# Memory attention and feed-forward on one core: cross-partition steps of batches 2 to 7 sent through DRAM

## The chip, the core and the metric

One core of one Trainium2 chip runs the whole program. The time is the device time of one execution in microseconds. Engines: TensorE (PE, with its weight loads as PEld), VectorE (DVE), ScalarE (ACT), GpSimd (POOL) and SyncE (SP), which issues the DMAs.

## The reference

`setup_inputs()` draws q, k and v of [8 batches, 8 heads, 576 positions, 64], phi of [8, 8, 576, 32] and two weights, 512 x 2048 and 2048 x 512. All are float32 but the weights, which come as float64 and are turned into float32 in the opening (steps `i{j}` and `o{j}`, ACT and DVE).

```python
a = softmax(phi, axis=2)                          # over the 576 positions
k_m = einsum('bhsm,bhsd->bhmd', a, k)             # 32 memory keys of 64 a head
v_m = einsum('bhsm,bhsd->bhmd', a, v)
scores = (1.0 / sqrt(64)) * q @ k_m.transpose     # [576, 32] a head
attn = softmax(scores, axis=-1)
x = (attn @ v_m), heads side by side              # 4608 rows of 512
h = x @ w_in;  g = maximum(0.01 * h, h)
return g @ w_out                                  # 4608 x 512, float32
```

## The kernel before

Attention's last product and the first weight are folded: for each batch the kernel multiplies v_m by w_in (`fold_products`, steps `W{b}{j}.p`) and applies the result to the attention weights. The feed-forward part runs over groups of rows. The first groups (`G` 0 to 2) are worked in units `P`/`V`/`C`/`L`/`O` of two feature blocks, the later ones in units `p`/`v`/`s`/`c`/`l`/`d`: `p` is the up product (PE, L1118), `v` the leaky activation (ACT, L1134), `s` sums (DVE, L1155), `c` and `l` a high and a low float16 part (ACT L1159, DVE L1163), `d` the down product (PE, L1186). `x`, `z` combine and store a finished group; `z` issues four DMAs for each of its two tiles (`send`, L1053).

The order is written out by hand: `OPENING` and `LATER` are lists of step names, and each engine (SP's DMA queue too) runs its own share of a list in that order. A step that waits holds everything behind it on its engine.

A batch's attention, `attention(b, ...)`, puts partition = (head of a pair g, 64 rows) x 4 pairs `hh`. Its steps, with the engines:

- `phi`, `kv0` to `kv3`, `q0`, `q1`: loads on SP (L539, L550, L570).
- `A1` (DVE, L579): maxima of phi over 9 positions in each partition. `A2` (PE, L593) transposes them, `A3` (DVE, L600, L603) reduces over 64 partitions' values and makes two diagonals, and `B0` (PE, L609) multiplies ones by them, so that each partition has its head's maxima in PSUM (`pb`).
- `B10` subtracts them (DVE, L618), `B20` exponentiates (ACT, L624), `B3` sums (DVE, L636).
- `C10` (PE, L658) multiplies by keys and values, `C2` (PE, L672) transposes the sums, `C30` makes factors (DVE, L681 to L686). `C3k` (ACT, L693) writes the scaled keys, each row of 32 repeated three times; `C31` (DVE, L704) writes the scaled values.
- `C4` (DVE, L712, L339, L341): the values' absolute sums, their maximum in each partition and a diagonal of it. `D2` (PE, L346) multiplies ones by the diagonal; `D4` (DVE, L351 on) takes the maximum over all partitions as a power of two.
- `D10` (PE, L723): four transposes of the repeated keys, 128 x 96 each. `D3` (ACT, L740): copy to `kT`, in which partitions 0 to 31, 32 to 63 and 64 to 95 hold the same rows. `D11`, `D5`, `D6`: the values, transposed and split.
- `Q0`, `Q1` (DVE, L776): q transposed in blocks. `E1` (PE, L797): the scores, which need all three copies in `kT` and q. `E20` to `E22` (DVE, L811) and `S01` to `S08`: softmax.

Batches 0 and 1 are float32 in the fold (`b < FB`, `FB = 2`) and belong to `OPENING`.

Of the kernel before, what the change touches and what calls it, by code (L numbers as in the profile page):

```python
# [45 lines left out]
o1.y0 o1.h0 u0.O0 o1.ld1 u0.P1 a0.S17 i1.y0 o0.t1 o1.y2 u1.V1 u0.V1 i1.h0 i1.t0 i1.h1 i1.y1
i1.t1 i2.ld0 i1.y2 i1.h2 o1.y1 o1.t0 o1.h1 u1.O0 u0.O1 o1.h2 i2.ld1 o2.ld0 i1.t2 f01.1 i2.h0
i2.y0 i2.y1 a0.S18 i2.h1 i2.t1 i2.ld2 f01.2 o2.y0 o1.t1 o2.ld1 o1.t2 o2.ld2 u1.O1 i2.t0 u2.P1
o2.h0 o2.t0 u2.P0 i2.y2 i2.h2 a1.phi i2.t2 a1.kv1 a1.q0 a1.kv0 f02.1 u2.V0 u2.O0 o2.y1 o2.h1
o2.t1 u3.P1 a1.kv2 o2.y2 o2.h2 a1.kv3 a1.A1 u2.V1 u3.P0 o2.t2 i3.ld0 f02.2 a1.q1 a1.A2 a1.A3  # L50
u4.P1 a1.B0 u3.V1 u4.P0 a1.B10 u3.V0 i1.b a1.B20 u3.O0 u4.V0 u5.P0 i2.b a1.B3 a1.C10 i3.ld2
a1.Q0 i3.ld1 a1.C2 u5.V0 o0.b o1.b u2.O1 u3.O1 i3.y0 u5.P1 u4.V1 a1.C30 a1.C31 a1.C4 a1.D2 o2.b
i3.h0 a1.C3k a1.D10 a1.Q1 i3.y2 i3.h2 a1.D11 a1.D4 i3.t2 a1.D3 a1.E1 o3.ld0 a1.D5 o3.y0 i3.y1
u4.O0 i3.h1 i3.t0 u5.V1 o3.ld2 u5.O0 a1.E20 i3.t1 o3.h0 o3.t0 a1.E21 i3.b ci.1 o3.ld1 a1.E22
a1.S11 f03.1 o3.y1 a1.S01 a1.S02 a1.S03 a1.S04 u4.O1 o3.y2 o3.h2 ci.2 f03.2 a1.S12 ci.3 ci.4 e.
o3.h1 o3.t1 a1.S05 u6.P0 u6.V0 a1.S13 a1.S06 a1.S07 u6.P1 u7.P0 a1.S14 a1.S15 o3.t2 w0.2 u6.O0
a1.S16 o3.b w1.1 u7.V0 co.1 co.2 u7.O0 w1.2 co.3 u6.V1 co.4 u5.O1 o0.k0 a1.S08 o0.k1 o0.k2
u7.P1 e2. o0.l0 u7.V1 o0.l1 u6.O1 a1.S17 a1.S18 o0.l2 u7.O1
# [16 lines left out]
o1.m2 o1.s3 V12.1 o1.n2 o2.k0 C12 W13.p o2.k2 o2.l0 a2.B0 W13.h1 P13.0 W13.h0 W13.l1 P13.1
W13.l0 V13.0 o2.k1 L12 P14.0 V13.1 o2.l2 O11.0 o1.m3 o2.l1 V14.0 C13 o2.s0 P14.1 L13 o2.m0
O11.1 V14.1 o1.n3 o2.n0 o2.s1 P15.0 C14 o2.m1 O12.0 o2.s2 V15.0 o2.n1 o2.m2 L14 P15.1 o2.s3
o2.n2 O12.1 o3.k1 a2.B10 V15.1 o3.k0 o3.l1 P16.0 o3.k2 o3.l0 a2.B20 O13.0 o3.l2 V16.0 C15 o2.m3
o3.s0 a2.C10 L15 o3.s1 a2.B3 P16.1 a2.q0 O13.1 V16.1 o3.s2 C16 o3.m1 a2.q1 a2.C2 i0.l2 o3.m2
P17.0 L16 o3.m3 O14.0 o3.m0 o3.n2 V17.0 a3.phi o3.n1 o3.n3 P17.1 a2.C30 O14.1 V17.1 a2.Q0  # L80
# [6 lines left out]
W21.l1 i3.k0 o2.n3 W22.p i3.l1 V22.1 O19.1 i3.k2 i3.l0 W22.h0 W22.h1 i3.l2 P23.0 C22 W22.l0
O20.0 V23.0 L22 W22.l1 a3.A1 W23.p P23.1 W23.h0 O20.1 W23.l0 V23.1 W23.h1 os2 C23 W23.l1 a3.A2
p0.0 L23 O21.0 v0.0 a3.A3 a3.B0 p0.1 a3.B10 O21.1 v0.1 a3.B20 p0.2 a3.B3 a3.C10 v0.2 O22.0
a3.q0 a3.C2 p0.3 a3.C30 a3.q1 O22.1 v0.3 a3.C3k a3.C31 s0 c0.0 a3.D10 a4.phi l0.0 c0.1 a3.D11  # L90
p1.0 a3.Q0 p1.1 v1.0 O23.0 v1.1 a3.D3 l0.1 a3.Q1 p1.2 O23.1 v1.2 a3.C4 a4.A1 p1.3 a3.D2 v1.3
p2.0 Z2.0 p2.1 Z2.1 s1 d0.0 Z2.2 a4.A2 v2.0 d0.1 v2.1 a3.D4 c1.0 d0.2 a4.A3 c1.1 p2.2 l1.0 d0.3
# [6 lines left out]
s5 d3.5 a4.q0 d3.6 p6.0 x3.3 p6.1 l5.0 v6.0 d4.0 a4.q1 v6.1 a4.B3 c5.1 d4.1 d4.2 z3.1 p6.2 l5.1
a4.C2 v6.2 d4.3 z3.0 a5.phi d4.4 a4.C30 p6.3 a4.Q0 d4.5 v6.3 a4.C3k d4.6 s6 p7.0 c6.0 a4.D10  # L100
v7.0 l6.0 p7.1 a4.D3 d5.0 a4.Q1 v7.1 c6.1 d5.1 d5.2 l6.1 p7.2 d5.3 v7.2 a4.C31 d5.4 a5.A1 a4.E1
a4.C4 p7.3 a5.kv2 a4.E20 d5.5 v7.3 a4.D2 c7.0 s7 d5.6 a5.kv0 p8.0 p8.1 l7.0 v8.0 d6.0 v8.1
a4.E22 a5.kv3 c7.1 d6.1 a4.E21 d6.2 l7.1 a4.D11 p8.2 a5.kv1 a4.S01 d6.3 v8.2 d6.4 a4.D4 p8.3
d6.5 a4.S02 v8.3 a4.D5 W32.p s8 d6.6 W32.h0 p9.0 W32.h1 p9.1 W32.l0 v9.0 d7.0 W32.l1 v9.1 d7.1
# [1269 lines left out]
```

## Time and profile before

| what | value |
|---|---|
| median of 3 runs | 663.42 us (661.62 to 663.84) |
| span of the profiled execution, first to last instruction | 661.5 us |
| the profiled execution's own device time | not given apart; the lowest of the runs is 661.62 us |
| PE busy | 642.5 us, 97% |
| DVE busy | 522.7 us, 79% |
| ACT busy | 396.3 us, 60% |
| POOL busy | 31.7 us, 5% |
| data moved by DMA | 60.38 MB |

A row of a timeline gives start, length, engine, line and operands, and in brackets how long the engine was idle before it and for whom. A row of the groups gives how often, the busy time, the mean length in ns, and the idle time before. Matmuls are pipelined: the length of one is longer than the distance to the next start.

### The profile page before, as it was taken

The page shows a single profiled execution, that of the slowest core. Times are in us where ns is not written, and L with a number is a line of the kernel's source. Part 1 is how long each engine was busy: PE and PEld are TensorE (multiplying, and loading weights), DVE is VectorE, ACT ScalarE, POOL GpSimd, SP SyncE. Part 2 cuts the span into 40 slices and gives each one's busy share as a digit, 9 for nine tenths or more (in the row PEclk, how much of TensorE's full clock was granted, in tenths as well). Part 3 has the DMA queues.
Part 4 walks back from the last instruction along what each step waited for, and adds up shares of the span by engine and source line. Part 5 has one row for each costly group of instructions (what it writes and reads, how often), then busy time and mean ns, then how long its engine had stood idle before and what let it go on. Part 6 is the DMA issues. An engine that isn't in the chain of part 4 may idle for free.

```text
span 661.5 us, 17591 instructions
## 1 busy us (share of the span) xinstructions
PE 642.5 (97%) x7592; PEld 482.2 (73%) x7592; DVE 522.7 (79%) x857; ACT 396.3 (60%) x677; POOL 31.7 (5%) x43
## 2 busy tenths in 40 slices
PE   6899999999999999999999999999999999999996
PEld 3345445665545787888888889887888888889883
DVE  5775789999994998989898965888877997575641
ACT  2797878674652655566546665655665466564552
POOL 0010021000110001001000020000010001000000
PEclk9799999999999999999999999999999999999999
DMA  9989803104601443611161101054104010100101
GB/s 251 406 334 323 277 3 95 63 1 110 190 1 38 116 149 73 172 43 33 39 182 68 34 1 33 8 136 146 33 1 106 2 34 7 28 25 11 33 2 48
DMA packets 31453, 60.38 MB, mean 91 GB/s; under 512 B 4240, under 2 KB 14480, under 8 KB 31376
## 3 DMA queue, kind: packets, MB, share of 16 engines
q1 hardware_dynamic: 31280, 59.13, 29.6%
q8 instruction: 59, 0.97, 0.6%
q10 hardware_dynamic: 96, 0.13, 0.1%
q14 instruction: 18, 0.15, 0.1%
HBM read 49.81 MB, written 9.44 MB: 90 GB/s over the span
## 4 chain that ended last, share of the span: by engine, by line
PE 86%; DVE 8%; DMA 2%; ACT 1%; issue 1%; SPq 0%; DVEq 0%; ACTq 0%
PE po L1186 30%; PE ph L1118 20%; PE po L1075 13%; PE ph L1007 7%; PE ph L1186 5%; PE pa L913 4%; DMA arena<-in_q_dram 2%; PE pa L797 2%; PE pa L658 2%; PE po L1220 1%; DVE arena L776 1%; DVE arena L1163 1%; DVE w_mem L952 1%; PE pa L1276 1%; DVE arena L443 0%
## 5 line engine op out<-in xcount | busy, mean ns | idle before, releaser
L1186 PEld LDWEIGHTS <-arena 128*128 128x128 f16 x2184 | 209.9, 98 | 33.2 <-issue 10.3
L1134 ACT ACTIVATE wi<-ph,g_sc 128x256 f32<-128x256 f32 (+1 forms) x224 | 99.2, 465 | 178.5 <-PE ph L1118 175.5
L1118 PE MATMUL ph<-a,w_mem 128*128 128x256 f16 (+3 forms) x1440 | 145.3, 246 | 0.7 <-ACT wi L1134 0.5
L1118 PEld LDWEIGHTS <-w_mem 128*128 128x128 f16 x1440 | 114.6, 98 | 14.3 <-issue 3.4
L1186 PE MATMUL po<-wo,arena 128*128 128x256 f16 x936 | 122.2, 273 | 1.2 <-issue 1.2
L1186 PE MATMUL po<-arena 128*128 128x256 f16 x936 | 122.2, 273 | 0.0
L1075 PE MATMUL po<-wo,arena 128*128 128x512 f16 (+1 forms) x384 | 111.1, 434 | 0.4 <-DVE arena L1028 0.4
L1163 DVE TENSOR_TENSOR arena<-arena 128x1024 f16<-128x1024 f32 x52 | 63.9, 1228 | 23.8 <-ACT arena L1159 23.7
L1163 DVE TENSOR_TENSOR arena<-wi,arena 128x768 f16<-128x768 f32 (+1 forms) x60 | 53.6, 893 | 10.1 <-ACT arena L1159 10.1
L1155 DVE TENSOR_TENSOR arena<-wi 128x256 f32<-128x256 f32 x104 | 41.0, 436 | 24.3 <-ACT wi L1134 23.0
L1159 ACT CAST arena<-arena 128x1024 f16<-128x1024 f32 x52 | 54.5, 1047 | 5.9 <-DVE arena L1155 5.9
L1007 PE MATMUL ph<-a,w_mem 128*128 128x192 f16 (+2 forms) x304 | 52.2, 317 | 0.7 <-DVE a L856 0.7
L1075 PEld LDWEIGHTS <-arena 128*128 128x128 f16 x288 | 27.7, 98 | 30.3 <-DVE arena L1028 0.9
L1159 ACT CAST arena<-wi 128x768 f16<-128x768 f32 (+1 forms) x60 | 46.6, 776 | 1.6
L1155 DVE TENSOR_TENSOR arena<-wi,arena 128x256 f32<-128x256 f32 x104 | 45.8, 440 | 1.8
L880 POOL TENSOR_TENSOR a<-t,a 128x384 f16<-128x384 f32 x22 | 24.1, 1120 | 438.2 <-ACT a L875 438.2
L1186 PE MATMUL ph<-wo,arena 128*128 128x256 f16 x312 | 42.6, 273 | 0.0
L1075 PEld LDWEIGHTS po<-wo,arena 128*128 128x128 f32 x96 | 17.7, 190 | 21.4 <-issue 19.0
L913 PE MATMUL pa<-wi,vT 64*32 64x512 f16 (+1 forms) x704 | 28.9, 420 | 0.4 <-ACT vT L746 0.4
L1014 ACT ACTIVATE arena<-ph,g_sc 128x384 f32<-128x384 f32 x32 | 18.4, 576 | 16.7 <-PE ph L1007 16.6
L1007 PEld LDWEIGHTS <-w_mem 128*128 128x128 f16 x240 | 20.7, 98 | 9.4 <-issue 3.4
L776 DVE STREAM_TRANSPOSE arena<-arena 96x1536 f32<-96x1536 f32 x14 | 24.8, 1768 | 3.1 <-PE pa L658 2.6
(204 smaller groups left out, 771.7 us busy)
## 6 DMA issues: line engine op xcount, KB each, us to landing
arena<-in_q_dram SPq DMA_DIRECT2D x16, 576.0 KB, 6.5
out_dram<-obs SPq DMA_DIRECT2D x142, 64.0 KB, 1.7
arena<-in_k_dram SPq DMA_DIRECT2D x28, 288.0 KB, 4.9
arena<-in_v_dram SPq DMA_DIRECT2D x28, 288.0 KB, 5.1
arena<-in_moe_w_in_dram SPq DMA_DIRECT2D x12, 512.0 KB, 9.1
arena<-in_moe_w_out_dram SPq DMA_DIRECT2D x8, 768.0 KB, 6.7
arena<-in_phi_dram SPq DMA_DIRECT2D x7, 576.0 KB, 5.5
arena<-in_moe_w_in_dram SPq DMA_DIRECT2D x8, 256.0 KB, 8.3
```

The costliest lines, as they stand in the source:

```text
L776: nc.vector.transpose(flat, ld["q", g].rearrange("p hh j d -> p (hh j d)"))
L880: nc.gpsimd.tensor_tensor(lo[:, tb], t2[:, tb], hi[:, tb], ALU.subtract)
L913: nc.tensor.matmul(pf[g][cols, :], lhs, rhs, start=(n == 0), stop=(n == len(passes) - 1), tile_position=(g * D, hh * M),)
L1007: nc.tensor.matmul(ph[:, t0:t0 + n * SB], lhs, rhs, start=(m == 0), stop=(m == len(seq) - 1))
L1014: nc.scalar.activation(dst, ph, AF.Prelu, scale=sc, alpha=SLOPE)
L1075: nc.tensor.matmul(po, lhs, rhs, start=(f == 0 and m == 0), stop=(f == NQ * NF - 1 and m == len(seq) - 1),)
L1118: nc.tensor.matmul(ph[:, t0:t0 + n], lhs, rhs, start=(m == 0), stop=(m == len(seq) - 1))
L1134: nc.scalar.activation(dst, ph, AF.Prelu, scale=g_sc2[:, j:j + 1], alpha=SLOPE)
L1155: nc.vector.tensor_tensor(gt[:, x], y, z, op)
L1159: nc.scalar.copy(dst[:, 0], src)
L1163: nc.vector.tensor_tensor(dst[:, 1], src, dst[:, 0], ALU.subtract)
L1186: nc.tensor.matmul(acc, g[:, x, s, u], rhs, start=(h == 0 and j == 0 and u == 0 and m == 0), stop=(j == NQ - 1 and u == 1 and m == 2), ski ...
```

## The change

For batches 2 to 7 (`far`) three things cross partitions otherwise; batches 0 and 1 keep the old steps, and `OPENING` holds the same steps in the same order.

```diff
+    dram = ctx.enter_context(tc.tile_pool(name="dram", bufs=2, space=bass.MemoryType.DRAM))
...
+    def max_row(src):
         m = sm.tile([P, 1], F32, name="m1")
         nc.vector.tensor_reduce(m, src, AX.X, ALU.max)
+        return m
+
+    def max_diag(src):
+        m = max_row(src)
         diag = sm.tile([P, P], F32, name="mdiag", bufs=1)
         nc.vector.tensor_scalar_mul(diag, ident, m)
         return diag
...
+        far = b >= FB
...
+        if far:
+            @step("A2")
+            def _():
+                t = att.tile([P, HP, 32], F32, name="r1k", bufs=2)
+                nc.vector.transpose(
+                    t.rearrange("p hh x -> p (hh x)"), var["mx"].rearrange("p hh m -> p (hh m)")
+                )
+                var["mx4"] = mx4 = sm.tile([P, HP], F32, name="mx4")
+                nc.vector.tensor_reduce(mx4, t, AX.X, ALU.max)
+
+            @step("A4")
+            def _():
+                d = dram.tile([P, HP], F32, name="d_mx")
+                nc.sync.dma_start(d, var["mx4"])
+                var["mb"] = mb = att.tile([P, 2 * M * HP], F32, name="r1k", bufs=2)
+                for g in range(NG):
+                    row = d[g * D:(g + 1) * D].rearrange("p (o hh) -> o (p hh)", o=1)
+                    nc.sync.dma_start(
+                        mb[g * D:(g + 1) * D], row.broadcast_to([D, 2 * M * HP])
+                    )
+
+            @step("A3")
+            def _():
+                two = var["mb"].rearrange("p (i m hh) -> p i hh m", i=2, hh=HP)
+                var["pb"] = pb = att.tile([P, HP, M], F32, name="r1k", bufs=2)
+                nc.vector.tensor_tensor(pb, two[:, 0], two[:, 1], ALU.max)
+        else:
...
         @step("C3k")
         def _():
-            var["x_k"] = x_k = att.tile([P, NG, ND, NB, 32], F32, name="x_k")
+            x_k = att.tile([P, NG, ND, NB, 32], F32, name="x_k")
+            if far:
+                both = x_k.rearrange("p g db tb x -> p (g db tb x)")
+                var["x_k"], var["kS"] = both[:, 0:P], both[:, P:2 * P]
+                for g in range(NG):
+                    nc.scalar.activation(
+                        var["x_k"][:, g * D:(g + 1) * D], var["pk"][g][:, 0:D], AF.Copy,
+                        scale=var["r2"][:, 1, g:g + 1],
+                    )
+                return
+            var["x_k"] = x_k
...
-            var["vdiag"] = max_diag(l1)
+            if far:
+                var["m1"] = max_row(l1)
+            else:
+                var["vdiag"] = max_diag(l1)
...
         @step("D10")
         def _():
+            if far:
+                var["pkT"] = ps_a.tile([P, P], F32, name="pa")
+                nc.tensor.transpose(var["pkT"], var["x_k"], ident)
+                return
...
-        @step("D2")
-        def _():
-            var["pm"] = spread(var["vdiag"])
-
-        @step("D3")
-        def _():
-            var["kT"] = kT = att.tile([CP, NG, ND, P], F32, name="kT")
-            nc.scalar.copy(kT, var["pkT"])
+        if far:
+            @step("C5")
+            def _():
+                d = dram.tile([P, 1], F32, name="d_m1")
+                nc.sync.dma_start(d, var["m1"])
+                var["pm"] = sm.tile([P, P], F32, name="mdiag", bufs=1)
+                nc.sync.dma_start(
+                    var["pm"], d.rearrange("(o p) x -> o (p x)", o=1).broadcast_to([P, P])
+                )
+
+            @step("D3")
+            def _():
+                nc.scalar.copy(var["kS"], var["pkT"])
+
+            @step("D12")
+            def _():
+                d = dram.tile([P, P], F32, name="d_k")
+                nc.sync.dma_start(d, var["kS"])
+                var["kT"] = kT = att.tile([CP, NG, ND, P], F32, name="kT")
+                for tb in range(NB):
+                    nc.sync.dma_start(
+                        kT[tb * 32:(tb + 1) * 32],
+                        d.rearrange("(g db x) c -> x g db c", g=NG, db=ND),
+                    )
+        else:
...
```

So `A2` becomes a block transpose and a reduction on DVE; `A4` writes 128 x 4 numbers to DRAM and reads each head's 256 of them into its 64 partitions; `A3` becomes one maximum of 128 columns; `B0` is gone. `C4` loses its diagonal, `C5` writes 128 numbers and reads all of them into every partition, and `D2` is gone. `C3k` writes each key row once, `D10` is one transpose of 128 x 128, `D3` copies its 128 columns to SBUF, and `D12` writes them to DRAM (64 KB) and reads them into `kT` three times. All nine DMAs of a batch are on SP.

`LATER` is a new list of the same steps besides these. The stretches from before `D10` to `E1` in batches 4, 5 and 6, as they now read:

```
batch 4: ... a4.B3 c5.1 d4.1 l5.0 d4.2 v6.1 z3.1 d4.3 p6.2 l5.1 a4.C2 v6.2 a5.phi d4.4 a4.C30 p6.3
  a4.Q0 os3 d4.5 z3.0 v6.3 a4.C31 a4.C3k d4.6 a4.D10 s6 p7.0 c6.0 l6.0 p7.1 a4.D3 a4.D12 d5.0 a4.Q1
  v7.0 v7.1 c6.1 d5.1 d5.2 p7.2 d5.3 v7.2 l6.1 d5.4 a5.A1 p7.3 a4.E1 a4.C4 a4.C5
batch 5: ... z5.1 a5.B3 d12.1 z5.0 d12.2 p14.2 d12.3 v14.2 a5.C2 d12.4 a6.phi p14.3 a5.C30 d12.5 a5.Q0
  v14.3 s14 a5.C3k a5.Q1 p15.0 a5.D10 a5.D3 c14.0 d12.6 l14.0 c14.1 v15.0 p15.1 a5.C31 d13.0 l14.1
  v15.1 a5.D12 d13.1 d13.2 d13.3 p15.2 p15.3 v15.2 a5.C4 a5.C5 a6.A1 d13.4 a5.E1
batch 6: ... a6.C3k d25.4 p27.3 a6.C4 a6.C5 a6.D10 v27.3 c27.0 l26.1 s27 a6.D11 d25.5 a6.D3 a6.D12
  d25.6 l27.0 c27.1 p28.0 a6.D4 p28.1 v28.0 d26.0 v28.1 a6.D5 d26.1 a6.Q1 d26.2 p28.2 p28.3 d26.3
  d26.4 a6.D6 v28.2 a7.A1 a6.E1
```

Elsewhere the list moves steps by a few places, `A3` comes after `A2` and `A4` with other DVE steps in between, and `D4` likewise after `C4` and `C5`.

More of the change, by code (lines that the diff above doesn't have):

```diff
@@ L46 @@
[L46 to L57, printed above, removed]
@@ L75 @@
[L75 to L80, printed above, removed]
@@ L87 @@
[L87 to L92, printed above, removed]
@@ L99 @@
[L99 to L104, printed above, removed]
@@ L184 @@
+d52.0 z15.0 z15.1 p54.1 d52.1 v54.1 p54.2 c54.0 d52.2 v54.2 l54.0 p54.3 d52.3 v54.3 p55.0 c54.1
+d53.0 l54.1 v55.0 p55.1 d53.1 v55.1 p55.2 c55.0 d53.2 l55.0 v55.2 p55.3 d53.3 v55.3 d54.0 c55.1
+l55.1 d54.1 d54.2 d54.3 d55.0 d55.1 d55.2 d55.3 end
 """
@@ L588, in attention @@
             steps[f"{name}A1"] = lambda: max_phi(0, HP)
-        @step("A2")
-        def _():
-            var["pt"] = pt = ps_a.tile([P, NG, D], F32, name="pa")
-            nc.tensor.transpose(
-                pt.rearrange("p g x -> p (g x)"), var["mx"].rearrange("p hh m -> p (hh m)"), ident
-            )
-        @step("A3")
-        def _():
-            mx2 = sm.tile([P, NG], F32, name="mx2")
-            nc.vector.tensor_reduce(mx2, var["pt"], AX.X, ALU.max)
-            var["diag"] = diag = att.tile([P, NG, P], F32, name="r1k", bufs=2)
-            for g in range(NG):
-                nc.vector.tensor_scalar_mul(diag[:, g, :], ident, mx2[:, g:g + 1])
```

263 lines of the change are left out of this document (151 added, 112 removed).

## The prediction

> **What bounds the kernel now.** I read the page's busy times and its chain first, then the stages, then the instructions around each piece that the change takes away.
>
> ```profile
> span 661.5 us, 17591 instructions
> PE 642.5 (97%) x7592; PEld 482.2 (73%) x7592; DVE 522.7 (79%) x857; ACT 396.3 (60%) x677; POOL 31.7 (5%) x43
> PEclk9799999999999999999999999999999999999999
> PE 86%; DVE 8%; DMA 2%; ACT 1%; issue 1%; SPq 0%; DVEq 0%; ACTq 0%
> ```
>
> The core's time by stages (busy time of PE, PEld, DVE, ACT, POOL, then clock, DMA share, GB/s):
>
> ```profile
> 104.00:170.00 66.00, 65.57 (x688) 39.85 (x687) 64.75 (x96) 44.07 (x72) 0.22 (x2) 1.00 0.30 86
> 290.00:350.00 60.00, 59.72 (x870) 51.56 (x868) 53.64 (x87) 36.55 (x64) 3.75 (x4) 1.00 0.31 86
> ```
>
> TensorE (PE) is busy for 65.57 of 66 and 59.72 of 60 us at full clock, and 86% of the chain is PE. From 104 us on, where batches 2 to 7 are worked, an instruction taken from PE's order is worth the distance to the next start, and whatever makes PE wait costs its full length. VectorE (DVE) is as full only from 104 to 170 us (64.75 of 66).
>
> **What PE loses.** PE's timeline, batch 7 first, then the same steps in batches 4, 5 and 6 (start, length, line):
>
> ```profile
> 477.88 0.27 PE L593 MATMUL pa<-ident,r1k 128*128 128x128 f32 x1
> 477.99 0.82 PE L1186 MATMUL po<-arena 128*128 128x256 f16 x6
> ...
> 482.78 0.44 PE L609 MATMUL pa<-r1k,ones 128*64 128x128 f32 x4
> 483.15 0.83 PE L1186 MATMUL po<-arena 128*128 128x256 f16 x6
> ...
> 512.75 0.60 PE L723 MATMUL pa<-ident,x_k 128*96 128x128 f32 x4
> 513.18 1.47 PE L1186 MATMUL po<-arena 128*128 128x256 f16 x12
> 514.49 0.49 PE L1118 MATMUL ph<-a,arena 128*128 128x256 f16 x3
> 514.82 0.49 PE L1118 MATMUL ph<-a,obs 128*128 128x256 f16 x3
> 515.74 0.49 PE L346 MATMUL pa<-mdiag,ones 128*128 128x128 f32 x2 [0.42 <-DVE mdiag L341]
> ...
> 268.95 0.60 PE L723 MATMUL pa<-ident,x_k 128*96 128x128 f32 x4
> 269.68 0.81 PE L1118 MATMUL ph<-a,w_mem 128*128 128x256 f16 x6
> ...
> 336.54 0.60 PE L723 MATMUL pa<-ident,x_k 128*96 128x128 f32 x4
> 337.42 0.81 PE L1118 MATMUL ph<-a,w_mem 128*128 128x256 f16 x6 [0.28 <-ACT wi L1134]
> ...
> 345.28 0.39 PE L346 MATMUL pa<-mdiag,ones 128*128 128x128 f32 x2
> 345.50 0.27 PE L731 MATMUL pa<-ident,x_v 128*128 128x128 f32 x1
> ...
> 440.17 0.62 PE L723 MATMUL pa<-ident,x_k 128*96 128x128 f32 x4
> 441.00 0.46 PE L346 MATMUL pa<-mdiag,ones 128*128 128x128 f32 x2 [0.21 <-DVE mdiag L341]
> ```
>
> Matmuls overlap, so I price by starts, not by lengths. A2 (one transpose) holds PE for 477.99 - 477.88 = 0.11 us. B0 (two products, four instructions) holds it for 483.15 - 482.78 = 0.37. D10 (four transposes) holds it for 0.43; one stays at 0.11, so 0.32 goes. D2 holds it for 345.50 - 345.28 = 0.22 where nothing disturbs it. Together 0.11 + 0.37 + 0.32 + 0.22 = 1.02 us a batch, 6.1 us over six batches.
>
> With D2 goes its wait for DVE's diagonal. In batch 7 three products started 0.33 apart from 514.49 to 514.82, so D2 could have started at 515.15 and did at 515.74: 0.59 lost. In batch 6 four transposes from 440.17 should end at 440.60 and D2 starts at 441.00: 0.4. I add 0.2 for the other four and take 1.2 us in all, zero and 1.5 as ends. After D10 in batch 5, PE stands 337.42 - 336.54 - 0.43 = 0.45 us behind ScalarE (ACT), which is busy with the copies of the keys; in batch 4 it is 269.68 - 268.95 - 0.43 = 0.3. The lighter copies below should win back about half of these 0.75: 0.4, ends 0 and 0.75. What PE gains: 6.1 + 1.2 + 0.4 = 7.7 us, ends 6.1 and 8.4.
>
> **DVE and ACT.** Groups by line and shape:
>
> ```profile
> L600 DVE TENSOR_REDUCE mx<-pa 128x2 f32<-128x128 f32 x8 | 2.2, 280 | 1.1 <-PE pa L593 1.1
> L603 DVE TENSOR_SCALAR r1k<-ident,mx 128x128 f32<-128x128 f32 x16 | 3.9, 284 | 0.4
> L341 DVE TENSOR_SCALAR mdiag<-ident,m 128x128 f32<-128x128 f32 x8 | 2.3, 287 | 0.3
> L811 DVE STREAM_TRANSPOSE t<-pa 128x384 f32<-128x384 f32 x24 | 12.7, 560 | 0.8 <-PE pa L797 0.6
> L712 DVE TENSOR_REDUCE l<-x_v 128x2 f32<-128x128 f32 x8 | 2.0, 254 | 0.0
> L693 ACT ACTIVATE x_k<-pa,r 128x192 f32<-128x192 f32 x14 | 5.1, 417 | 0.3 <-DVE r L686 0.3
> L740 ACT COPY kT<-pa 96x512 f32<-96x512 f32 x8 | 4.6, 578 | 2.0 <-PE pa L723 2.0
> L746 ACT COPY vT<-pa 128x128 f32<-128x128 f32 x2 | 0.5, 264 | 0.2 <-PE pa L731 0.2
> ```
>
> DVE drops the reduction of 280 ns, two diagonals of 284 and one of 287: 1.14 us a batch. It gains a transpose of 128 columns, a reduction like L712's (254), and a maximum of 128 columns like L603's (284). The transpose lies between a third of L811's 560 and all of it; I take 300, so 0.84 us. DVE is lighter by 0.3 us a batch. B1 (the subtraction) and the reduction in D4 only read another place; I cost that at nothing. On ACT two copies of 417 ns shrink to 64 columns (at least L746's 264 halved, at most 417; I take 300), and D3 goes from 578 to L746's 264: 0.55 us a batch. Neither engine is on the path after 170 us, so none of this enters the sum beyond the 0.4 above.
>
> **The round trips.** Nothing in this trace writes to DRAM and reads back, so each hop is bounded by its nearest row: stores of 64 KB for the write, input loads of 288 KB for the read.
>
> ```profile
> L1053 SPq DMA_DIRECT2D out_dram<-obs x142: 314/422/1871, 105.1 to 658.2; - x142
> ...
> DMA to landing us min/median/max: 1.6/1.7/3.6
> ...
> L550 SPq DMA_DIRECT2D arena<-in_k_dram x28: 328/384/1805, 48.5 to 451.3; - x28
> ...
> DMA to landing us min/median/max: 2.7/5.3/11.5
> ```
>
> A write: 1.7 us (1.6 to 3.6). A read of at most 64 KB: above a store's 1.6, below 2.7, the quickest load of 288 KB; I take the middle, 2.2, with 5.3 as the far end if small reads fare like loads. Each issue holds the SP queue for 0.42 us. So A4 (write, two reads) lasts 1.7 + 0.4 + 2.2 = 4.3 us, C5 (write, one read) 3.9, D12 (write, three reads) 1.7 + 0.8 + 2.2 = 4.7. SP serves its list in order: while it waits for a write, all later loads and stores stand behind it. Per batch that is some 1.7 us three times and nine issues of 0.42. In the rows below SP issues eight stores and a load and has nothing to do before and after, and loads are listed long before their use, so I cost that at nothing; if a load became late, its reader on DVE would wait by as much.
>
> A3 and D4 make DVE wait for A4 and C5. Batch 3 has the closest A3, with about 4.6 us of DVE work listed after A2 against 4.3. Batch 6 has the closest D4, about 3.7 against 3.9 behind C4. D5 on ACT follows D4, so a late bound also holds activations there. What hides small misses is DVE's lead over PE:
>
> ```profile
> 338.33 1.23 DVE L1163 TENSOR_TENSOR arena<-arena 128x1024 f16<-128x1024 f32 x1
> ...
> 347.60 0.82 PE L1186 MATMUL ph<-wo,arena 128*128 128x256 f16 x6
> ```
>
> This operand is ready at 339.56 and its products start at 347.60, 8 us later. If that lead were gone, each miss would cost its length.
>
> E1 makes PE itself wait for D12. Counting PE's blocks (twelve products of 256 take 514.49 - 513.18 = 1.31 us above, so six take 0.66) between D10 and E1 in the new order gives the cover: 8.8 us in batch 2, 13.8 in 3, 5.9 in 4, 5.9 in 5, 7.3 in 6, 10.6 in 7. Batches 2, 3 and 7 cover the 4.7 us and the copies before it. The others also have the next phi load just ahead on the same queue:
>
> ```profile
> 331.45 4.75 SPq L1053 DMA_DIRECT2D out_dram<-obs x8
> 336.31 0.41 SPq L539 DMA_DIRECT2D arena<-in_phi_dram  x1
> ...
> 435.90 0.39 SPq L539 DMA_DIRECT2D arena<-in_phi_dram  x1
> ```
>
> Batch 5: eight stores and phi end on SP at 336.7, 0.2 us after D10. D12's write then goes out at about D10 + 0.8, right behind 576 KB, so I give it the slow 3.6: landed at 4.4, last read at 4.4 + 0.8 + 2.2 = 7.4, cover 5.9: 1.5 us lost. Batch 4: phi is earlier, but four stores (z3.0, 1.7 us) come between and a cast of ACT stands before D3: write at 1.4, landed at 3.6 (2.2, mild traffic), last read at 6.6: 0.7 lost. Batch 6: SP has C5 before D12. Phi left at D10 - 4.3; C4 ends at about D10 + 0.5, C5's write takes 2.1 (phi is nearly in) and lands at 2.6, its read is out at 3.0, D12's write lands at 4.8, last read 7.8 against 7.3: 0.5 lost. Sum 2.7 us; ends 0 and 2.7 + 3 x 3.1 = 12 (reads of 5.3).
>
> **Sum.** 661.5 - 7.7 + 2.7 = 656.5 us of span. The median of the runs shown, 663.42, is 1.9 above the span; what lies around the span and the scatter of 661.62 to 663.84 make this up. So 658.4 us, 0.8% faster. A difference of 0.3% (2 us) is what a measurement can tell here.
>
> **Rivals.** (1) All round trips are hidden, since the reads land in 1.6 to 1.9 us and the phi load doesn't delay the writes. Then the whole 7.7 to 8.4 us shows: 655.0 to 655.7. For it: undisturbed stores land in 1.7 and the misses are all under 1.5. Against: the 3.6 among the stores. (2) The other side: the reads fare like loads, E1 becomes the new stop of PE, and the kernel is slower. With 5.3 us a read, batches 4, 5 and 6 lose 9.3 more: 667.7. It cancels the gain at 2.2 + 5.0 / 3 = 3.9 us a read. For it: the reads pass the same 16 engines as phi, and loads take 5.3 in the median. Against: those are 288 KB each and up to eight in a row. (3) In between, reads of about 3.7 us leave no difference: 662.9. (4) DVE is the bound from 104 to 170 us, so batch 2's 1.0 us doesn't appear: 659.4, inside the first case's range; DVE's lighter load speaks against it.
>
> The stores' spread from 1.7 to 3.6 is what rival 2 rests on. [...]
>
> **How the numbers follow.** Forecast 0.56 (own range 656.0 to 661.3), rival 1 0.23, rival 3 0.12, rival 2 0.09. Faster 0.56 + 0.23 = 0.79, same 0.12, slower 0.09. The range starts at 654.0, a little under rival 1, and ends at 663.0, which leaves out rival 2 and some of both edges.
>
> **What would show it.** PE's busy time falls by about 6 us and L346, L593 and L609 keep only batches 0 and 1. L723's counterpart is one transpose a far batch. E1's first matmul shows a wait for a DMA of about 1.5 us in batch 5 and under 1 in 4 and 6. Small reads land in about 2.2 us, writes in 1.7. DVE shows short waits for DMA at A3 and D4, without PE waiting after them. The prediction is wrong if reads take 4 us or more, if a far E1 waits over 3 us, or if the new order makes PE wait at places that have nothing to do with the round trips.

## The result and the profile after

The changed kernel takes 696.75 us in the median (695.55 to 697.21) beside 663.45 us (661.62 to 663.84): ratio 1.0509, 95% interval 1.0484 to 1.0535. It is 33 us slower, outside the range and on the other side of no change. The profiled execution spans 694.8 us. From its page, the span, the busy times, the granted clock by slices and the beginning of the chain:

```profile
span 694.8 us, 17550 instructions
PE 651.2 (94%) x7532; PEld 484.9 (70%) x7532; DVE 517.1 (74%) x851; ACT 390.6 (56%) x677; POOL 32.1 (5%) x43
PEclk9999999999999999999999999997999989999999
PE 67%; DMA 13%; DVE 12%; ACT 4%; issue 2%; another core or an unknown queue 1%; SPq 1%; POOL 0%; DVEq 0%; ACTq 0%; POOLq 0%
```

PE runs 60 instructions fewer (7592 to 7532), as the change says, and yet is busy for 8.7 us more (642.5 to 651.2). Fewer products are busy for longer if they run at a lower clock (six of 128x256 take 0.82 us from 346.35 on, at a clock of 1.00, and 1.49 from 476.04 on, at 0.50), and the clock row has two dips in the middle that were not there before. (A slice is 17 us long. Seen more finely, by windows of the trace, the granted clock is at 0.50 or 0.51 in five stretches: 3.4 us each from 235.9, 300.8 and 352.0 us on, 10.2 from 468.0 and 6.8 from 553.3.) The chain, 86% PE, 8% DVE and 2% DMA before, now has 67% PE, 13% DMA and 12% DVE. So there are two losses: PE waits, and afterwards it is slow.

The DMA issues of the new steps (KB each, and the median time from issue to landing in us):

```profile
r1k<-d_mx SPq DMA_DIRECT2D x12, 64.0 KB, 2.8
kT<-d_k SPq DMA_DIRECT2D x18, 64.0 KB, 1.9
d_k<-x_k SPq DMA_DIRECT2D x6, 64.0 KB, 3.3
d_mx<-mx SPq DMA_DIRECT2D x6, 2.0 KB, 1.8
mdiag<-d_m SPq DMA_DIRECT2D x6, 64.0 KB, 5.6
d_m<-m SPq DMA_DIRECT2D x6, 0.5 KB, 7.2
```

The maxima and the keys are near their forecast: writes 1.8 and 3.3 us, reads 2.8 and 1.9. The odd pair is C5's, and its odd member is the smallest transfer of the list: 512 bytes take 7.2 us to be written, and reading them back takes 5.6. With the issue of the read in between, C5 lasts about 13 us.

Who waits for it, from the list of who waited for whom (us in total, times, longest):

```profile
DVE pv L352 <- DMA mdiag<-d_m: 26.6, 5, 7.9
ACT vT L832 <- DVE sv L826: 24.9, 5, 7.6
PE ph L1189 <- ACT wi L1205: 11.4, 9, 3.8
PE pa L868 <- DVE vT L837: 5.7, 1, 5.7
PE pa L868 <- DMA kT<-d_k: 4.8, 1, 4.8
```

This is one wait handed on. DVE stands at D4 (L352), ACT behind it at D5 (L832), and PE behind ACT's next activations or behind D6 (L837). Batch 7 in the timeline (start, length, engine, line; in brackets the idle time before and what ended it):

```profile
541.03 0.38 SPq L783 DMA_DIRECT2D d_m<-m  x1
...
547.71 0.51 PE L868 MATMUL pa<-arena,kT 32*32 32x192 f32 x4
548.27 0.34 SPq L785 DMA_DIRECT2D mdiag<-d_m  x1
552.03 0.29 DVE L352 TENSOR_REDUCE pv<-mdiag 128x1 f32<-128x128 f32 x1 [7.87 <-DMA mdiag<-d_m]
...
552.92 0.37 ACT L832 ACTIVATE vT<-pa,sv 128x128 f16<-128x128 f32 x1 [7.65 <-DVE sv L826]
553.55 0.34 DVE L837 SCALAR_TENSOR_TENSOR vT<-pa,sv,vT 128x128 f16<-128x128 f32 x1
553.94 0.53 PEld L868 LDWEIGHTS pa<-arena,kT 32*32 32x32 f32 x29 [6.10 <-DVE vT L837]
```

C5's write goes out at 541.03 and its read only 7.24 us later. E1 starts at 547.71 and stops after four products: its next score tile needs a `ps_a` buffer that D11's `px` holds until D5 and D6 have read it, and these wait for the bound. PE stands for 6 us for a number that it doesn't use.

The stretch with that wait and the one behind it, and the same for batch 6 (busy time of PE, PEld, DVE, ACT, POOL, then clock, DMA share, GB/s):

```profile
465.00:471.00 6.00, 1.18 (x10) 0.65 (x7) 2.27 (x5) 1.45 (x4) 0.00 (x0) 0.75 0.18 53
471.00:476.00 5.00, 5.00 (x102) 3.23 (x101) 3.80 (x8) 0.48 (x1) 0.00 (x0) 0.50 0.31 79
...
548.00:553.50 5.50, 0.22 (x4) 0.00 (x0) 1.32 (x5) 0.58 (x2) 0.00 (x0) 0.99 0.04 12
553.50:560.50 7.00, 6.56 (x110) 4.51 (x110) 5.14 (x12) 1.35 (x3) 0.00 (x0) 0.52 0.01 2
```

After each long wait PE is fully busy again, at a clock of 0.50 and 0.52. That is where the extra busy time comes from.

### The profile page after: what moved, and what is told of

It is laid out like the page before. It is cut to its first block, busy times and chain, and to the rows that moved or that the text cites. A ratio compares the mean times of both kernels' runs of the same rounds, so it can differ in the third digit from the quotient of the medians.

```text
span 694.8 us, 17550 instructions
## 1 busy us (share of the span) xinstructions
PE 651.2 (94%) x7532; PEld 484.9 (70%) x7532; DVE 517.1 (74%) x851; ACT 390.6 (56%) x677; POOL 32.1 (5%) x43
## 4 chain that ended last, share of the span: by engine, by line
PE 67%; DMA 13%; DVE 12%; ACT 4%; issue 2%; another core or an unknown queue 1%; SPq 1%; POOL 0%; DVEq 0%; ACTq 0%; POOLq 0%
PE po L1257 24%; PE ph L1189 17%; PE po L1146 8%; DMA d_m<-m 5%; PE ph L1078 5%; PE ph L1257 4%; PE pa L984 4%; PE pa L687 2%; DMA mdiag<-d_m 2%; DMA arena<-in_moe_w_in_dram 2%; DVE arena L847 2%; PE pa L868 1%; PE po L1291 1%; DMA arena<-in_moe_w_out_dram 1%
## 5 line engine op out<-in xcount | busy, mean ns | idle before, releaser
L1257 PEld LDWEIGHTS <-arena 128*128 128x128 f16 x2184 | 213.0, 99 | 34.9 <-issue 9.0
L1189 PE MATMUL ph<-a,w_mem 128*128 128x256 f16 (+3 forms) x1440 | 147.0, 248 | 10.5 <-ACT wi L1205 10.5
L1189 PEld LDWEIGHTS <-w_mem 128*128 128x128 f16 x1440 | 116.0, 99 | 26.0 <-issue 13.9
L1257 PE MATMUL po<-wo,arena 128*128 128x256 f16 x936 | 126.4, 279 | 0.0
L1146 PEld LDWEIGHTS <-arena 128*128 128x128 f16 x288 | 27.8, 98 | 33.3 <-issue 4.1
L1226 DVE TENSOR_TENSOR arena<-wi,arena 128x256 f32<-128x256 f32 x104 | 43.8, 421 | 1.8
L984 PE MATMUL pa<-wi,vT 64*32 64x512 f16 (+1 forms) x704 | 30.4, 428 | 1.7 <-ACT vT L817 1.2
L868 PE MATMUL pa<-arena,kT 32*32 32x192 f32 x672 | 18.0, 383 | 12.4 <-DVE vT L837 5.7
L1017 ACT ACTIVATE w_mem<-pa 128x512 f16<-128x512 f32 x40 | 22.4, 595 | 9.8 <-PE pa L984 8.9
L1023 DVE SCALAR_TENSOR_TENSOR w_mem<-pa,w_mem 128x512 f16<-128x512 f32 x40 | 26.3, 680 | 0.9 <-ACT w_mem L1017 0.9
```

What stands on the lines that cost most here:

```text
L868: nc.tensor.matmul(psc[tb][cols, g, :], var["kT"][rows, g, db, cols], var["qT", g][rows, hh, :, db, :], start=(db == 0), stop=(db == ND - ...
L984: nc.tensor.matmul(pf[g][cols, :], lhs, rhs, start=(n == 0), stop=(n == len(passes) - 1), tile_position=(g * D, hh * M),)
L1023: nc.vector.scalar_tensor_tensor(tiles(t[:, 1]), w(g), ws, tiles(t[:, 0]), ALU.mult, ALU.subtract)
L1146: nc.tensor.matmul(po, lhs, rhs, start=(f == 0 and m == 0), stop=(f == NQ * NF - 1 and m == len(seq) - 1),)
L1189: nc.tensor.matmul(ph[:, t0:t0 + n], lhs, rhs, start=(m == 0), stop=(m == len(seq) - 1))
L1226: nc.vector.tensor_tensor(gt[:, x], y, z, op)
```

## The experiments

Three terms are used throughout. "Waits of PE" are the sum of all gaps over 0.25 us between the starts of two products beyond the first one's own length, from 104 us to the end: 15.7 us before and 44.3 after. The sum also counts the length of small products that start side by side, so only its differences between kernels mean something; the profile's own list of PE's waits adds up to some 5 us before and 8 in versions 1 and 5, which is the same difference. "Order of before" and "new order" are the two lists `LATER`. "Version 3" is the kernel of experiment 3, and so on.

**1. Bound back on PE.** The changed kernel and its order, without C5 and with D2 again:

```
-            @step("C5")
-            def _():
-                d = dram.tile([P, 1], F32, name="d_m1")
...
+            @step("D2")
+            def _():
+                var["pm"] = spread(var["vdiag"])
```

> The changed kernel with v's bound back on TensorE (D2 and the diagonal instead of C5); maxima and keys still go through DRAM, and the new order stays. Theory A: the bound's round trip (write 7.2 us, read 5.6 us in the trace of after) is the whole loss, by DVE and ACT standing in D4 and D5, then PE, then the halved clock. Then 663.4 - 6 x (0.11 + 0.37 + 0.32) = 658.6 us plus up to 3 us of waits in E1: 657 to 662, mean granted clock 0.99. Rival B: the three trips and the new order share the loss. Then at least 672 us, and clock under 0.985.

Measured: 662.3 us (660.87 to 664.05), ratio 0.9999 (0.9979 to 1.0019), 0.3 us above theory A's range and 10 below rival B's. Without C5 all 33 us are gone. The trips of the maxima and of the keys, in the same order, cost nothing net, but the 4.8 us of PE work that they save (0.11 + 0.37 + 0.32, six times) don't show either. Waits of PE are 19.3 us, 3.6 more than before, the largest group of them this:

```profile
PE ph L1190 <- ACT wi L1206: 4.4, 6, 2.1
```

None of them names a DMA. ACT is late at places where the new order has put other work of ACT or DVE ahead.

**2. The bound alone.** The order of before and all of its steps, with C5 right behind C4 and D2 gone, for instance in batch 3:

```
-a3.C4 a4.A1 p1.3 a3.D2 v1.3
+a3.C4 a3.C5 a4.A1 p1.3 v1.3
```

> The kernel before, in its own order, with one part of the change: v's bound through DRAM, C5 right behind C4, no D2. Theory A: about the whole loss appears: 685 to 700 us, clock 0.97 to 0.98, D4 waiting some 5 us a batch. Rival B: 675 us or less.

Measured: 706.5 us (704.67 to 707.93), ratio 1.0665 (1.0636 to 1.0694), beyond the range of theory A too. The order of before leaves even less between C4 and D4: DVE stands at D4 for 40.5 us, beside 26.6 in the changed kernel. Waits of PE are 52.2 us, and the largest is the buffer of `px` again:

```profile
PE pa L869 <- DVE vT L838: 17.0, 3, 7.7
```

**3. The bound used later.** The changed kernel, its order altered alone: C5 behind D12, and D4 to D6 (in batches 3, 6 and 7 also D11 and the fold products) at least 13 us of PE work behind C4, for instance in batch 2:

```
-... C18 Z1.2 O16.0 a2.D11 a2.S01 ... a2.S02 i1.k1 a2.D4 a3.kv1 ... a2.D5 P20.0 ... a2.D6
+... a2.D12 a2.C4 a2.C5 P18.1 ... a2.D11 a2.S01 ... O18.0 a2.D4 a2.D5 a2.D6 i1.l1 a2.S08
```

> The changed kernel with all three trips, and only the order altered: C5 stands behind D12 on SP, and D4, D5, D6 (with D11 and the fold's W steps in batches 3, 6 and 7) come at least 13 us of PE work behind C4. Theory A says that what hurts is the wait behind too short a cover: 656 to 661 us and clock 0.99. Rival C: SP itself, held 7 us a batch by the slow write, delays loads, stores and E1, so that even a covered trip costs: at least 668 us.

Measured: 671.8 us (667.81 to 673.88), ratio 1.0153 (1.0123 to 1.0182). With nearly the same trip (writes of 6.2 us, reads of 5.4) merely covered, 25 of the 33 us are back, and in the profiled execution no slow stretch of the clock is left in the middle. The forecast of full cover was too good, and the time lies where rival C had put it. The trace doesn't bear C out: SP does stand behind C5's writes for 39.5 us, but after 104 us no wait of PE, DVE or ACT for a DMA is longer than 0.3 us. Waits of PE are 27.8 us, and they have moved to the steps that I had shifted, ACT first:

```profile
PE ph L1190 <- ACT wi L1206: 8.1, 12, 2.1
PE pa L764 <- ACT x_k L725: 2.0, 1, 2.0
```

The profiled execution took 667.81 us at a mean clock of 0.997; the other three took 671.60 to 673.88 at 0.988 to 0.994. What made them 4 to 6 us longer is not in a trace, and stays open.

**4. The trips by themselves.** A kernel of write and read pairs on an otherwise empty chip, each behind the one before, four times over. It leaves out the reference's whole computation. The form of rows of 4 bytes:

```
+        nc.sync.dma_start(d[:, 0:src_cols], src)
...
+            row = d[0:n].rearrange("p x -> (p x)").rearrange("(o y) -> o y", o=1)
+            nc.sync.dma_start(t, row.broadcast_to([P, dst]))
```

> Leaves out the whole computation: only hops through DRAM, one after another on an otherwise idle queue, four times each: 128 rows of 4, 8, 16, 64 and 512 bytes, 4-byte rows at a pitch of 64 and 512 bytes, four rows of 4 bytes, one row of 512 bytes, each read back. Theory A1 (row size): 4-byte rows land in about 7 us at any pitch, 16-byte rows in about 1.8. Theory A2 (rows that share a block of memory): 4-byte rows land in about 7 us when packed and about 2 at a pitch of 512 bytes; 8-byte rows lie between. Rival A3 (the kernel's own traffic): all land in 1.5 to 2.5 us here. For the reads: one row of 512 bytes read by all 128 partitions takes 4 to 6 us if the shared source slows it, 2 if traffic did.

From its list of DMA issues (128 rows written each time; 0.5 KB are rows of 4 bytes, 1.0 KB of 8, 2.0 KB of 16, packed without a gap; `w4at` are rows of 4 bytes at a distance of 64 or 512 bytes; `t_one` is one row of 512 bytes read into 128 partitions, `t_f` one of 16 bytes; the 64 KB `t_w` are four reads of 128 different rows of 512 and four of C5's form). The last number is the median of the landings on record, one or two of the four of most forms; that of the 64 KB `t_w` is of 128 different rows:

```profile
t_w<-d_w SPq DMA_DIRECT2D x8, 64.0 KB, 1.8
...
t_one<-d_one SPq DMA_DIRECT2D x4, 64.0 KB, 3.1
d_w4at<-s_w4at SPq DMA_DIRECT2D x8, 0.5 KB, 1.4
...
d_w<-s_w SPq DMA_DIRECT2D x4, 0.5 KB, 6.9
d_w<-s_w SPq DMA_DIRECT2D x4, 1.0 KB, 3.0
d_w<-s_w SPq DMA_DIRECT2D x4, 2.0 KB, 2.2
...
t_f<-d_f SPq DMA_DIRECT2D x4, 2.0 KB, 2.5
```

The write is slow without any traffic, so theory A3 (contention) falls. It isn't the size of a row either (A1): rows of 4 bytes take 6.9 us packed and 1.4 us at a distance of 64 bytes. It is how close the rows lie in DRAM (A2): of 128 rows, 16 to every 64 bytes cost 6.9 us, 8 rows 3.0, one row 1.4. With 4 rows the 2.2 is a single landing; by the start of the read behind it, four of five such writes took 1.4 us and one 2.2. A short row as such costs nothing here: by the same measure rows of 4 bytes at a distance took 1.4 us, rows of 64 bytes 1.4 and rows of 512 bytes 1.5. Why close rows are slow, no run shows. What the trace does show is where the time lies (DVE, POOL, clock, DMA share, GB/s):

```profile
53.28:54.48 1.20, 0.00 (x0) 0.00 (x0) 1.00 0.06 0
54.48:60.28 5.80, 0.00 (x0) 0.00 (x0) 1.00 0.00 0
```

The packed write was issued at 53.28 and the read that waits for it at 60.29. The DMA engines have work for it only in the first 1.2 us, at a share of 0.06; for the other 5.8 us their share is 0.00 and the write is still awaited. The same number of rows at a distance, issued at 90.15, was over after 1.4. So neither the number of rows nor work of the DMA engines that the trace shows makes the difference. On the read side one shared source row takes 3.1 us where 128 different rows of the same size take 1.8.

**5. Four rows instead of 128.** The changed kernel and its order, with the bound reduced before it leaves the chip: DVE spreads the row maxima over 32 columns, turns the 32x32 blocks and takes the maximum again, and C5 carries 4 numbers.

```
-                var["m1"] = max_row(l1)
+                m1 = max_row(l1)
+                nc.vector.tensor_scalar_mul(w[:, 0:32], ones[:, 0:32], m1)
+                nc.vector.transpose(w[:, 32:64], w[:, 0:32])
+                nc.vector.tensor_reduce(w[:, 64:65], w[:, 32:64], AX.X, ALU.max)
...
-                nc.sync.dma_start(d, var["m1"])
+                nc.sync.dma_start(d, var["w"][0:P:32, 64:65])
```

> The changed kernel with its order, but v's bound made compact before it leaves the chip: VectorE spreads the 128 row maxima over 32 columns, turns the 32x32 blocks, and takes the maximum again, so that one value stands for each block of 32 rows; C5 then writes 4 rows of 4 bytes and reads one row of 16 bytes into every partition. Three short VectorE instructions a batch are added. Theory (packed 4-byte rows are slow to write and one 512-byte row shared by 128 partitions is slow to read, and nothing else of C5 costs): in the bare trips such a write took about 1.6 us and such a read about 2.5 us, so C5 ends 4 to 5 us after C4 instead of 13, PE's long waits around D4 to D6 go, the granted clock is 0.99 again, and the time is 659 to 665 us, that is at or a little below the 662 of the version with the bound on PE. Rival (the place of the D4 to D6 steps in the new order is wrong for any trip through DRAM, however short): waits of 2 to 4 us stay and the time is 675 us or more.

Measured: 660.95 us (659.49 to 661.86), ratio 0.9969 (0.9952 to 0.9987), 0.3% faster than before, 36 us faster than the changed kernel. Its page and its new DMAs:

```profile
span 658.0 us, 17568 instructions
PE 635.1 (97%) x7532; PEld 477.4 (73%) x7532; DVE 520.5 (79%) x869; ACT 391.4 (59%) x677; POOL 31.9 (5%) x43
PEclk9999999999999999999999999999999999999999
...
mdiag<-d_m SPq DMA_DIRECT2D x6, 2.0 KB, 2.7
```

This gives the cleanest account of the loss, because PE has the same 7532 instructions as in the changed kernel. The spans differ by 694.8 - 658.0 = 36.8 us. Of these, 651.2 - 635.1 = 16.1 are PE's busy time, the same products at a lower clock (some 3 of it in the opening, where the clock is 0.97 up to 104 us in the changed kernel, while version 5's mean over its whole span is 1.000), and 20.7 are PE's idle time. DVE, with three more instructions a batch, has nothing to say in it.

**6. The pause by itself.** 21 groups of float16 products with ScalarE copies between them, for which the next group waits. It leaves out the reference's whole computation. `n` goes from 1 to 8000 and back:

```
+        for _ in range(GROUP):
+            nc.tensor.matmul(acc, w, r, start=True, stop=True)
...
+            nc.scalar.copy(x[:, 0:1], acc[:, 0:1])
+            nc.scalar.copy(y[:, 0:n], x[:, 0:n])
+            nc.scalar.copy(r[:, 0:1], y[:, 0:1])
```

> This measures the granted clock after a pause of TensorE by itself and leaves the reference's whole computation out: 21 groups of 160 float16 products of 128x512 (about 35 us each), and between them ScalarE copies that the next group waits for, from a bare 0.5 us to about 8 us, once in rising and once in falling order. Theory H (a pause of 2.8 us and more, not the work around it, halves the clock afterwards): no half-clock stretch behind pauses under about 2 us, a stretch of 3.4 us or more behind every pause above 3 us, longer behind the longest. Rival (the half clock of the changed kernel comes with what its other engines do, not with the pause): full clock throughout, whatever the pause.

Pauses are given from one start to the next, 0.2 us of which is the first product. No slow stretch followed those of 0.63 to 2.24 us; of the two of 2.8 us one was followed by one, of the two of 3.41 us one, and from 3.99 us on every one. Each slow stretch behind a pause was 3.4 or 6.8 us long. How equal pauses differ shows in stretches of 3.4 us laid on the edges of the slow ones (columns as above):

```profile
197.10:200.50 3.40, 1.05 (x5) 0.39 (x4) 0.00 (x0) 2.25 (x3) 0.00 (x0) 1.00 0.00 0
200.50:204.00 3.50, 3.41 (x9) 1.19 (x9) 0.00 (x0) 0.04 (x1) 0.00 (x0) 0.51 0.00 0
234.60:238.00 3.40, 2.32 (x11) 0.98 (x10) 0.00 (x0) 1.01 (x2) 0.00 (x0) 1.00 0.00 0
238.00:241.50 3.50, 1.55 (x8) 0.72 (x8) 0.00 (x0) 1.86 (x2) 0.00 (x0) 1.00 0.00 0
```

The pause of 2.83 us lay in one stretch, left PE busy for 1.05 of 3.40 us in it, and the next stretch ran at 0.51. The pause of 3.41 us lay across two, left 2.32 and 1.55, and neither was followed by a slow one. That the place of a pause between such edges decides is my reading. It fits the changed kernel, whose slow stretches of 3.4, 6.8 and 10.2 us start 64.9, 51.2, 116.0 and 85.3 us apart, to 0.1 us 19, 15, 34 and 25 times 3.41. There less than 2.83 us was enough: PE idle for 2.10 us, at p15.1, all of them in one stretch. Version 5 has the same 2.10 us idle, from 333.57 to 335.67, of which 1.97 lie in the stretch of the last row:

```profile
348.50:351.95 3.45, 1.35 (x13) 1.07 (x11) 3.42 (x6) 2.29 (x4) 0.00 (x0) 1.00 0.60 183
351.95:355.40 3.45, 3.45 (x19) 2.46 (x17) 3.35 (x6) 0.13 (x1) 0.00 (x0) 0.51 0.27 60
...
333.70:337.10 3.40, 1.43 (x14) 1.28 (x14) 3.37 (x7) 2.15 (x4) 0.00 (x0) 1.00 0.53 174
```

The first two rows are of the changed kernel, the last of version 5, where the 3.4 us behind it ran at 1.00. So for these two waits the border lies near 1.4 us of work in 3.4, and one of the five slow stretches stands behind a wait that isn't C5's. PE's busy time alone isn't the whole measure. In the changed kernel the two longer slow stretches go on behind 3.4 us with PE busy for 3.41 us (from 471.42 on) and 2.81 (from 553.34 on), almost all of it E1's 32*32 products at a clock of 0.50; and in the opening a slow stretch stands behind 1.51 us (from 24.27 on), and before the change one behind 2.19 (from 14.33 on). The rival, other engines' work as the cause, falls, since here the slow stretches come with DVE, POOL and the DMA at 0.00.

**7. Where the saved PE work goes.** Single parts of the change in the order of before. The maxima alone (A4 behind A2, A3 right ahead of B10), for instance in batch 5:

```
-v12.2 a5.A2 d10.4 ...
+v12.2 a5.A2 a5.A4 d10.4 ...
...
-d11.0 a5.B10 v13.1
+d11.0 a5.A3 a5.B10 v13.1
```

> The kernel before with its own order and one part of the change alone: in batches 2 to 7 phi's maxima go through DRAM (A2 writes follow A1, A4's reads follow A2, A3 stands right ahead of B10, B0's products are gone). Theory O (the trips of the maxima are hidden, and what the version with the bound on PE lost, it lost in waits that the new order makes): the 2.9 us of PE work saved shows, 660.0 to 661.5 us, ratio 0.995 to 0.998, and PE's waits after 104 us stay within 1 us of the 15.7 us of before. Rival D (the trips by DMA themselves make new waits, whatever the order): 662.5 us or more, and waits of PE on A3 or B10.

Measured: 663.41 us (661.78 to 665.61), ratio 1.0011 (0.9998 to 1.0024): theory O falls for this part. PE is rid of 2.9 us and waits 3.6 us more, at C10 (L687), behind the exponentials that the later A3 makes late. In batches 3 and 5 A3 itself is late because DVE waits there for A4's reads, so that here, as rival D has it, the trip is too long for its place:

```profile
PE pa L687 <- ACT arena L653: 2.4, 2, 1.9
...
DVE r1k L617 <- DMA r1k<-d_mx: 5.4, 2, 3.0
```

The keys alone, and both. In these two the delayed scores of batches 2, 4, 5 and 6 come behind loads of the next batch into the queries' area, so that part of the scores is made from other data. Batch 4, the same in both:

```
-a4.D3 d5.0 ... a5.A1 a4.E1 a4.C4 p7.3 a5.kv2 a4.E20 d5.5
+a4.D3 a4.D12 d5.0 ... a5.A1 a4.C4 p7.3 a5.kv2 d5.5 v7.3 c7.0 s7 d5.6 a5.kv0 p8.0 a4.E1 p8.1 a4.E20
```

> The kernel before with its own order and one part of the change alone: in batches 2 to 7 the repeated rows of keys go through DRAM (D12 right behind D3); the scores from E1 on, and the D steps that stand behind E1 in batches 2, 4, 5 and 6, are put 1.3 to 4.6 us of PE work later, so that at least 6.5 us lie between D3 and E1. Theory O (hidden trips, a loss only by the new order): the 1.9 us of PE work saved shows, 661.0 to 662.5 us, ratio 0.996 to 0.999. Rival D (the trips or the later scores make new waits): 663 us or more, with PE waiting at E1 on kT's transfers.

> The kernel before with its own order and two parts of the change: maxima and keys through DRAM as in the two kernels run beside it, v's bound left on PE. Theory O: the two gains add up, 658 to 660.5 us, ratio 0.993 to 0.997; this would be the best version so far. Rival D: within 0.3% of before, as the same two parts were in the new order (662.3 us beside 662.25).

Measured: 678.54 us (ratio 1.0234, 1.0211 to 1.0257) and 677.41 us (1.0230, 1.0209 to 1.0252). The waits on those loads are in these times, so they say nothing of the trips. The keys alone once more, with the loads behind E1, in batch 4 (against the list above):

```
-p7.3 a5.kv2 d5.5 v7.3 c7.0 s7 d5.6 a5.kv0 p8.0 a4.E1 p8.1 a4.E20
+p7.3 d5.5 v7.3 c7.0 s7 d5.6 p8.0 a4.E1 a5.kv2 p8.1 a4.E20 a5.kv0
```

> The kernel before with its own order and the keys alone through DRAM, as in the run of the keys before, with one difference: the loads of the next batch's keys and values, which share an area with this batch's queries, stay behind E1. In the two runs with keys in the old order they had come ahead of it, so that the scores of batches 2, 4, 5 and 6 were partly made from the next batch's data and E1 waited for those loads. Theory O (hidden trips; what is lost is lost by an order that puts late work before PE): 661.0 to 663.0 us, within 0.3% of before or a little under, PE's waits at E1 below 1 us each. Rival D (the trip or the later scores cost PE more than the 1.9 us saved): 664.5 us or more.

Measured: 668.75 us (668.20 to 669.23), ratio 1.0088 (1.0070 to 1.0106). Slower, as rival D has it, but not where it looked: PE doesn't wait at E1 at all. It waits at the fold products (L985), since D4 to D6 had to move behind the later E1:

```profile
PE pa L985 <- DVE vT L838: 2.7, 1, 2.7
```

This wait leaves PE busy for 1.05 us of the 3.4 from 185.20 on, and the next 3.4 us run at a clock of 0.50. So no single part pays when it is put into the order of before by hand. What a trip needs is room, and in a full order the room is taken from another step.

**8. The short bound in the order of before.** The list of version 2 with the lines of version 5:

> The kernel before with its own order and one part alone: v's bound through DRAM in the four-row form, C5 right behind C4 where the 512-byte form cost 44 us. Theory (it was the length of the trip, 13 us beside 4 to 5): 660 to 665 us; about 2.5 us of PE work saved, at most some 1 to 2 us lost in batches 3, 6 and 7, where D4 follows C4 within 2.7 to 4.9 us of PE work. Rival (any trip through DRAM at this place costs PE): 675 us or more.

Measured: 664.78 us (663.55 to 667.10), ratio 1.0036 (1.0023 to 1.0050): 42 us less than version 2, with C5 at the same place. It was the length of the trip. It still costs 0.4% there, at scores that wait until D6 has read `px`:

```profile
PE pa L873 <- DVE vT L842: 2.7, 3, 1.8
```

**9. Four steps moved.** Version 5, with batch 4's C3k and D10, v15.0 and batch 7's C10 moved by a few places:

```
-d4.4 a4.C30 p6.3 a4.Q0 os3 d4.5 z3.0 v6.3 a4.C31 a4.C3k d4.6 a4.D10 s6 p7.0 c6.0
+d4.4 a4.C30 a4.C3k p6.3 a4.Q0 os3 d4.5 z3.0 v6.3 a4.C31 d4.6 s6 p7.0 a4.D10 c6.0
...
-d12.6 l14.0 c14.1 v15.0 p15.1
+d12.6 l14.0 v15.0 c14.1 p15.1
...
-a7.B3 a7.C10 d33.4
+a7.B3 d33.4 a7.C10
```

> The four-row version of the changed kernel with four steps of its order moved: batch 4's C3k ahead of its Q0 and its D10 behind p7.0, v15.0 ahead of c14.1, batch 7's C10 behind d33.4. These are the places at which PE still waited 1.6, 2.3 and 1.1 us. Theory (those waits belong to the new order and are what keeps the saved PE work from showing): 655 to 658.5 us, 3 to 5 us below the four-row version's 660.95. Rival (the waits only move to the next late engine): 659.5 to 662 us.

Measured: 658.78 us (657.54 to 660.87), ratio 0.9943 (0.9923 to 0.9963), the best version here. It is just outside the forecast: D10's wait is gone and p15.1's is 0.97 instead of 2.26 us. The third move missed its wait: the C10 that waits 1.1 us, at 429 us in both versions, is batch 6's, and batch 7's, at 501 and 503 us, waits in neither. And in batch 4 the later D10 makes E1 wait for its trip:

```profile
PE pa L873 <- DMA kT<-d_k: 1.2, 1, 1.2
```

Both theories hold in part: some of the wait was the order's, some only moved. The interval overlaps a little with version 5's.

## Why the prediction was wrong

**The step that failed is the price of C5.** "A write: 1.7 us (1.6 to 3.6)", "I take the middle, 2.2", "C5 (write, one read) 3.9". Measured: 7.2 and 5.6, with the issue some 13 us. The nearest rows were chosen by kilobytes; the stores of 64 KB have 128 rows of 512 bytes, C5 has 128 rows of 4 bytes in 512. Neither of the rows that it took has writes of 4 bytes a row, and yet 3.6 was its upper end for a write. An operation without any row of its own form needed a far wider end, and a wider range with it.

**The cover.** "What hides small misses is DVE's lead over PE ... 8 us later" was true of the lead and wrong of the cover. D5 stands on ACT in order, ahead of the activations that PE needs next, and D11's `px` holds one of three `ps_a` buffers until D6. The second way needs no lead to be used up: in batch 7 PE stops in the middle of E1. The prediction named ACT behind D4 but gave the wait no price.

**"Each miss would cost its length"** was too cheap: the five waits that left PE busy for 0.00 to 1.35 us of a stretch of 3.4 us cost half of the next 3.4, 6.8 or 10.2 us too, at a clock of 0.50. By versions 5 and 6 that is 13 to 16 of the 36.8 us. The term was missing altogether.

**What held.** PE's gain: 642.5 to 635.1 us of busy time in version 5, 7.4 us, with the opening's clock in it, against 6.1 from the instructions. The other writes and reads (1.8 and 3.3 against 1.7; 2.8 and 1.9 against 2.2); the keys' write, 3.3 us beside C5's slow one, took 2.1 in version 5. The loss at E1 was put too high: in version 5 no E1 waits for more than 0.5 us, against 2.7 us in the sum. In the changed kernel itself batch 6's E1 waits 4.8 us for `kT`, but that is C5 again: SP stands at C5's write while D12 is listed behind it.

```profile
464.73 0.33 SPq L785 DMA_DIRECT2D mdiag<-d_m  x1
465.50 0.32 SPq L796 DMA_DIRECT2D d_k<-x_k  x1
...
468.83 1.27 SPq L799 DMA_DIRECT2D kT<-d_k  x3
...
470.62 1.35 PE L868 MATMUL pa<-arena,kT 32*32 32x192 f32 x4 [4.82 <-DMA kT<-d_k]
```

**The order's own waits** were listed as what would make the prediction wrong, and they take most of the gain even without C5: 15.7 us of waits before, 19.3 in version 1 and 19.5 in version 5. That is why a kernel rid of 6 us of PE work is 2 us faster and not 6.

**The rivals.** Rival 2 had the sign, the wrong place (E1's reads) and the wrong size (667.7). Asked of D4 instead, with 13 us against a cover of some 4 in the closest batch, it would have priced the mechanism that decided.

What stays open: how much each of the two remaining trips is worth in an order made for it alone, and why a shared source row is read in 3.1 us by itself and in 5.6 us behind C5's write (from a row written in 4-byte pieces the bare trip also took 4.8, from 60.29 to 65.10 us, and the slice of its page from 56.6 to 62.3 us shows 0 GB/s).

## What to carry to other kernels

Price a transfer by its rows and how close they lie, not by its bytes: here 128 numbers, one to a partition, packed into 512 bytes of DRAM took 7.2 us to be written, beside 1.7 for a store of 64 KB. A short reduction that leaves four numbers (1.6 us by the start of the read behind it in the bare trips), or a distance of 64 bytes between the rows (1.4), brought it back to the others' price. Before a wait is called hidden, follow not only its reader but what stands behind it in order on each engine and which buffers stay held until it ends. On TensorE the waits that left it busy for 1.35 us or less of a 3.4 us stretch had 3.4 to 10.2 us at half the clock behind them in the changed kernel, and half of that is to be counted with the wait. The shortest idle time that did so was 2.10 us; the same 2.10 us did not in version 5.

## What the runs showed of the hardware

- 128 rows written to DRAM, in the bare trips: 6.9 us for packed rows of 4 bytes, 3.0 of 8, 1.4 or 2.2 of 16, 1.4 for 4-byte rows 64 or 512 bytes apart. In the packed form of 4 bytes the DMA share is 0.06 in the first 1.2 us and 0.00 in the last 5.8.
- One 512-byte row read into 128 partitions: 3.1 us, beside 1.8 for 128 different rows, and 2.5 for one row of 16 bytes.
- Granted clock, from 104 us on: 0.50 for 3.4, 6.8 or 10.2 us in the changed kernel, behind each of five stretches of 3.4 us in which PE was busy for 0.00, 0.00, 1.08, 1.21 and 1.35 us; 1.00 behind stretches with 1.52 and 1.71 us there (from 171.04 and 546.51 on) and with 1.43 in version 5. Once at 0.50, it stayed there behind stretches with 0.80, 2.81 and 3.41 us.
